# The last 64 keys' values of two head groups in one 64x64 quad, and the first unit's rest rows multiplied in place

## The chip, the cores and the metric

The kernel runs on one core of a Trainium2 chip. Its engines work side by side: TensorE (PE; its weight loads are listed as PEld), VectorE (DVE), ScalarE (ACT) and GpSimd (POOL); SyncE (SP) issues the DMAs. The metric is the time of one execution on the device in microseconds (us), lower is better. Before the change it is 1386.94 us, the median of three runs (1384.19 to 1387.12).

## The reference

Attention with normalised queries and keys, and a feed-forward block with a squared ReLU behind it, all in float32:

```python
q, k, v: (8, 12, 448, 64); g_q, g_k: (64,)
q_n, k_n = rmsnorm(q, g_q), rmsnorm(k, g_k)
attn = softmax(q_n @ k_n^T / sqrt(64))
a = attn @ v                                   # (8, 12, 448, 64)
x = a.transpose(0, 2, 1, 3).reshape(3584, 768)
out = relu(x @ w_in) ** 2 @ w_out              # w_in (768, 2048), w_out (2048, 768)
```

## The kernel before, in words

**Head groups.** A head group `i` is two heads (`e` = 0, 1) of one batch element; there are 8 x 6 = 48. For each group the kernel computes the scores transposed: keys on the 128 partitions, the 448 queries along the row. 448 keys are three chunks of 128 (`m` = 0, 1, 2) and a last one of 64 (`m` = NJ). Since 64 is half a chunk, the last chunks of an even group and of the odd group behind it share one tile: `score` (its matmuls are L444 and L455) writes the even group's to partitions 0 to 63 and the odd group's to 64 to 127, ACT takes the exponential (`weigh`, L463), and both are kept under the even group's key (`key_of`).

**Values.** `attend` (L527) multiplies the exponentials with the values into one PSUM bank, a pair of matmuls per chunk, one for each head (each fills 64 output partitions). For the last chunk the kernel has two ways. In the later units (`joint`, groups from 24 on) `attend_both` (L574) multiplies the shared tile's two halves in four 64x64 quarters of the PE array: the even group's into its own bank, the odd group's into a bank aside, which ACT copies to SBUF (`rests`) and DVE adds later. Before that, each group multiplies the whole shared tile (128 keys) with `lasts[i % 2]`, whose other 64 rows are zero, in a pair of matmuls like the other chunks (L545). `values_of` gives the order of the chunks: an odd group takes the last one first there.

**Stages.** Phase 1 (`visit_alone`) has nothing but attention for the first two batch elements, and weight preparation on DVE, ACT and POOL. A group is visited twice (`n` = 0, 1): scores and exponentials of two chunks, transposes of the next group's q and k (banks 7 and 6), the values of the group before; in the second visit the sums of the exponentials by matmuls with ones (`add_weights`, L594) as well. Then the feed-forward runs in four units (`ffn(u)`), a unit for two batch elements (896 rows), while the attention of the next unit's elements is visited in between (`visit_among` beside the first unit, `visit_whole` beside the later ones). Beside the first unit the sums of the exponentials are added on POOL (`additions`, L482) and their matmul (`denominators`, L611) goes into bank 3, half a visit ahead of the visit. q and k of the next group come in blocks and are transposed on DVE (`turn_blocks`, L367), q is scaled by the gains on ACT (L377).

**Units.** A unit has four blocks of the hidden dimension. The first half of a block is x times w_in (first unit: `first_products`, L1006; later units: `deep_products`, L1062), the second half the hidden rows times w_out (`second_products`, L1260). Both use a scheme of seven products in place of eight on 2x2 blocks (P1 to P7, with forms S1 to S4 of the left and T1 to T4 of the right operand; the S forms are made on POOL, `hidden_sum`, L1171). The second half takes rows in 128s: three tiles (`tt` = 0 to 2) for each of the two batch elements, 2 x 384 of the 2 x 448 rows. The last 64 rows of both elements of a unit are its *rest*, 128 rows that do not fit the 2x2 scheme alone. Before the change, the hidden rests of units 0, 1 and 2 go to DRAM (`keep_rests`, L1179), and the last unit fetches them block by block (`bring_rests`, L1201): rests of units 1 and 2 together make one 2x2 tile more (`tt` = NT), those of units 0 and 3 another (`tt` = NT + 1), seven products each. The last unit's tiles run in the order NT, 0, 1, NT + 1, 2.

**What sets the order.** All instructions are written in order by hand (`manual_schedule`); each engine runs its own in that order. A unit is a generator that yields a cost after each product (18 for a product of the first half of the first unit, 10 for one of the second half). `run(until)` draws products until their cost reaches a mark, and after each one it makes one sum of weight forms (`make_sum`, L1515, DVE and POOL in turn), sends some DMAs, starts a weight conversion if one is due (`late`), and runs a few queued tasks (turns, inverses, additions, normalisations). `place(u, x)` gives the mark of each visit. A conversion (`convert`) is a DMA of words (L1387, L1392), three ACT operations that split them (L1406, L1407, L1409), and on DVE L1420 and L1439 one step later; the conversions of a block end with the second w_out tile, whose T forms are four sums.

In the first unit's cost scale a block is 462 long (252 and 210); visits are marked at thirds of the first and thirds of the second half, and the conversions have eight dates in the second half and eight in the first 160 of the next first half.

## Time and profile before

| | |
|---|---|
| median of three runs | 1386.94 us (1384.19, 1386.94, 1387.12) |
| the profiled execution | 1384.19 us, its span 1382.4 us, granted PE clock 0.999 |
| PE busy | 1358.1 us (98%), 6304 records |
| DVE, ACT, POOL busy | 817.9, 608.7, 804.1 us |
| phase 1 | to about 129.5 us |
| beside the first unit | 129.5 to 480 us, PE busy 343.25 of 350.5 |
| later units with attention | 480 to 1060 us, PE busy 577.52 of 580 |
| the last unit | 1060 to 1382.4 us, PE busy 316.83 of 322.4 |
| values of the last chunk, pairs (L545 on `lasts`) | 96 records, 23.0 us busy |
| values of the last chunk, quads (L580) | 96 records, 14.0 us busy |
| second-half products (L1260) on hid, sums | 800 and 576 records, 285.6 and 205.8 us busy |

A float32 matmul is two records here. Records overlap, so a group's busy time is the union of its records, and the mean of one record is longer than its share of PE's time. In the order of time each line has the start, the length, the engine, the line of the kernel, and what ended the idle time before it in brackets. In a table of stages the columns are the stretch, its length, then busy time and number of instructions of PE, PEld, DVE, ACT and POOL, the granted clock, the DMA share and GB/s.

### The profile page before, as it was taken

How to read it: one execution, taken by the hardware profiler on the slowest of the kernel's cores; microseconds unless marked ns; L12 is line 12 of the kernel's file. 1: busy time of each engine (PE TensorE's matmuls, PEld its weight loads, DVE VectorE, ACT ScalarE, POOL GpSimd, SP SyncE). 2: the span in 40 equal slices, each digit the busy share in tenths (PEclk: the TensorE clock that was granted, in tenths of full speed). 3: DMA queues.
4: the chain of work that ended last, by engine and by line, in shares of the span. 5: the costliest groups of instructions: out<-in, count | busy, mean ns of one | idle time of the engine just before them, and what ended most of it. 6: DMA issues, size and time to landing. Idle time of an engine off the chain costs nothing.

```text
span 1382.4 us, 19667 instructions
## 1 busy us (share of the span) xinstructions
PE 1358.1 (98%) x6304; PEld 844.4 (61%) x6304; DVE 817.9 (59%) x1647; ACT 608.7 (44%) x1122; POOL 804.1 (58%) x810
## 2 busy tenths in 40 slices
PE   7999999999999999999999999999999999999998
PEld 3333444444444585867767675858676968677784
DVE  4786556867767755554557754555547523545454
ACT  6885477767665344333435243433332132202020
POOL 5568764746747886765859875765647440505040
PEclk9999999999999999999999999999999999999999
DMA  5566847869779685756658583847445724334132
GB/s 143 150 158 181 211 124 186 255 185 269 209 188 291 185 237 144 212 141 153 189 154 236 151 241 83 234 113 193 122 140 168 252 65 130 107 104 144 59 122 93
DMA packets 399429, 232.32 MB, mean 168 GB/s; under 512 B 273876, under 2 KB 361044, under 8 KB 398292
## 3 DMA queue, kind: packets, MB, share of 16 engines
q1 hardware_dynamic: 399024, 230.90, 59.4%
q8 instruction: 52, 0.85, 0.3%
q14 instruction: 61, 0.50, 0.1%
q10 hardware_dynamic: 292, 0.07, 0.0%
HBM read 172.49 MB, written 58.39 MB: 167 GB/s over the span
## 4 chain that ended last, share of the span: by engine, by line
PE 82%; DVE 5%; DMA 5%; ACT 3%; SPq 3%; issue 2%; POOL 1%; ACTq 0%; POOLq 0%; DVEq 0%
PE bank L1260 33%; PE bank L1062 25%; PE bank L455 4%; PE bank L559 4%; PE bank L444 4%; PE bank L545 4%; PE bank L1006 3%; DMA words<-in_moe_w_out_dram 2%; DMA qk<-in_k_dram 1%; PE bank L594 1%; DVE more L1475 1%; PE bank L620 1%; SPq L318 1%; DVE acc L1346 1%; PE bank L580 1%
## 5 line engine op out<-in xcount | busy, mean ns | idle before, releaser
L1062 PE MATMUL bank<-xT,in_sb 128*128 128x224 f32 x1344 | 288.2, 353 | 0.0
L1260 PE MATMUL bank<-out_sb,hid 128*128 128x384 f32 x800 | 285.6, 489 | 2.1 <-DVE acc L1346 2.1
L1062 PEld LDWEIGHTS bank<-xT,in_sb 128*128 128x128 f32 x1344 | 252.9, 190 | 10.6 <-ACT wT L463 5.6
L1346 DVE TENSOR_TENSOR acc<-acc,bank 128x384 f32<-128x384 f32 x300 | 160.0, 548 | 146.3 <-PE bank L1260 136.9
L463 ACT ACTIVATE wT<-bank,rr 128x448 f32<-128x448 f32 x288 | 163.9, 631 | 135.1 <-PE bank L444 95.9
L1260 PEld LDWEIGHTS bank<-out_sb,hid 128*128 128x128 f32 x800 | 149.8, 190 | 114.3 <-issue 9.5
L1260 PE MATMUL bank<-out_sb,sums 128*128 128x384 f32 x576 | 205.8, 489 | 1.7 <-DVE acc L1346 1.2
L204 POOL TENSOR_TENSOR rr<-ms,minus_half 128x8 f32<-128x8 f32 (+1 forms) x96 | 147.3, 1535 | 77.9 <-DVE ms L197 69.7
L1047 DVE TENSOR_TENSOR hid<-hid,bank 128x224 f32<-128x224 f32 x312 | 111.3, 384 | 84.9 <-PE bank L1062 79.6
L1260 PEld LDWEIGHTS bank<-out_sb,sums 128*128 128x128 f32 x576 | 108.1, 190 | 83.9 <-DVE acc L1346 4.8
L1006 PE MATMUL bank<-xT,in_sb 128*128 128x448 f32 x336 | 131.9, 546 | 0.3 <-DVE hid L1148 0.3
L1115 POOL TENSOR_TENSOR hid<-hid 128x448 f32<-128x448 f32 x24 | 27.3, 1142 | 176.4 <-DVE hid L1047 172.0
L482 POOL TENSOR_TENSOR sum<-sum,wT 128x448 f32<-128x448 f32 (+1 forms) x96 | 112.4, 1190 | 4.6 <-ACT wT L463 2.9
L455 PE MATMUL bank<-qT,kT 64*128 64x448 f32 (+1 forms) x492 | 104.4, 573 | 3.0 <-ACT qT L377 1.8
L1006 PEld LDWEIGHTS bank<-xT,in_sb 128*128 128x128 f32 x336 | 62.1, 190 | 69.3 <-issue 60.2
L482 POOL TENSOR_TENSOR sum<-wT 128x448 f32<-128x448 f32 x48 | 56.1, 1189 | 66.7 <-ACT wT L463 66.6
L1119 ACT ACTIVATE hid<-hid 128x448 f32<-128x448 f32 x96 | 55.0, 573 | 72.9 <-DVE hid L1047 48.4
L1059 ACT COPY hid<-bank 128x448 f32<-128x448 f32 x24 | 12.8, 533 | 144.6 <-PE bank L1062 144.6
L455 PEld LDWEIGHTS bank<-qT,kT 64*128 64x128 f32 (+1 forms) x492 | 35.6, 167 | 64.7 <-issue 36.2
L444 PE MATMUL bank<-qT,kT 64*64 64x448 f32 x552 | 75.1, 540 | 0.0
L1062 PE MATMUL bank<-more,in_sb 128*128 128x224 f32 x288 | 74.4, 353 | 0.0
L559 PE MATMUL bank<-wT,vt 64*64 64x448 f32 x576 | 73.3, 545 | 0.0
(148 smaller groups left out, 2063.2 us busy)
## 6 DMA issues: line engine op xcount, KB each, us to landing
out_sb<-out_forms SPq DMA_DIRECT2D x80, 384.0 KB, 5.0
in_sb<-in_deep SPq DMA_DIRECT2D x64, 384.0 KB, 4.0
in_sb<-in_deep SPq DMA_DIRECT2D x80, 256.0 KB, 4.0
words<-in_moe_w_in_dram SPq DMA_DIRECT2D x32, 384.0 KB, 4.0
words<-in_moe_w_out_dram SPq DMA_DIRECT2D x32, 384.0 KB, 3.6
out_forms<-out_sb SPq DMA_DIRECT2D x8, 1536.0 KB, 6.0
qk<-in_q_dram SPq DMA_DIRECT2D x96, 96.0 KB, 2.7
qk<-in_k_dram SPq DMA_DIRECT2D x96, 96.0 KB, 2.8
```

The source lines that it names most:

```text
L204: self.nc.gpsimd.tensor_tensor(out=self.rr[i][:, x, 0 : self.count(i)], in0=ms, in1=self.minus_half.to_broadcast(list(ms.shape)), op=ALU.pow,)
L444: nc.tensor.matmul(sc[ds(half * D, D)], lhsT=turned[i, 1][ds(e * D, D), ds(m * P + half * D, D)], rhs=turned[i, 0][ds(e * D, D), :], start ...
L455: nc.tensor.matmul(sc[some], lhsT=turned[p, 1][r, keys], rhs=turned[p, 0][r, :], start=True, stop=True,)
L463: nc.scalar.activation(new_weights((i, m), e), sc, AF.Exp, scale=rows.rr[i][:, 1, 2 * m + e : 2 * m + e + 1],)
L482: nc.gpsimd.tensor_tensor(out=sums[i, e][some], in0=left[some], in1=weights[key_of(i, m), e][some], op=ALU.add)
L545: nc.tensor.matmul(values_bank(i)[ds(e * D, D), :], lhsT=lasts[i % 2][mine, e, :] if m == NJ else values[i][:, m, e, :], rhs=weights[key_o ...
L559: nc.tensor.matmul(bank[ds(e * D, D), :], lhsT=values[i][keys, n, e, :], rhs=weights[(i, n), e][keys], start=n == 0, stop=n == NJ - 1 and ...
L1006: nc.tensor.matmul(ps, lhsT=w_sb[:, IN.index(left), c, :], rhs=forms[u, c][right], start=first and c == 0, stop=c == NK - 1, skip_group_ch ...
L1047: nc.vector.tensor_tensor(out=quarter(name, n), in0=quarter(base, n), in1=ps, op=ALU.add)
L1062: nc.tensor.matmul(ps, lhsT=left, rhs=right, start=start, stop=stop, skip_group_check=True)
L1260: nc.tensor.matmul(ps, lhsT=lefts[left][:, t, ts(tt, P)] if tt < NT else extra[tt - NT][left][:, t], rhs=w_sb[t][:, OUT.index(right), :], ...
L1346: nc.vector.tensor_tensor(out=acc, in0=acc, in1=ps, op=ALU.add)
```

## The change

1. `attend_both` is used for all groups. An even group's last chunk is multiplied together with the odd group's, four matmuls of 64 keys by 64 outputs: the even group's into its values bank, the odd group's into bank 6 in phase 1 and bank 2 beside the first unit. ACT copies that bank to `rests`; when the odd group is finished, DVE adds it to the bank and then multiplies with the inverse. The odd group's own values have three chunks, [0, 1, 2], so its second visit has one pair (beside the first unit) or none (phase 1). The order in which the sums are taken stays (`sums_of`). Both `lasts` tiles are loaded with the even group; their zero halves are no longer written.
2. The rests of the first and of the last unit are multiplied in their own unit by plain products, eight matmuls per block (`multiply_rest`): in the first unit at the head of each second half (three of four parts, then the fourth), in the last unit inside tile 0, whose order is `FIRST_OF_BLOCK`. Units 1 and 2 still keep theirs in DRAM, and the last unit still multiplies them as tile NT; tile NT + 1 is gone. The last unit's tiles run in the order 0, NT, 1, 2. The first and last unit hold one accumulator more.
3. The first unit's block is 502 long (252 and 250) in its cost scale; the visits are marked at equal distances over the whole unit, and the conversions are due every 31.4 without a break.

```diff
     def values_of(i):
         if i % 2:
-            return [0, 1, 2] if joint(i) else [NJ, 0, 1, 2]
+            return [NJ, 0, 1, 2] if shift else [0, 1, 2]
         return [0, 1, 2, NJ]
+
+    def sums_of(i):
+        return [NJ, 0, 1, 2] if i % 2 else [0, 1, 2, NJ]
...
         for n in some:
+            if n >= len(order):
+                continue
             m = order[n]
+            if m == NJ and not shift:
+                attend_both(i)
+                continue
             if joint(i):
-                if m == NJ:
-                    attend_both(i)
-                else:
-                    attend_halves(i, n)
+                attend_halves(i, n)
                 continue
...
     def attend_both(i):
-        other = banks[0][:, 0:S]
+        other = banks[0 if joint(i) else 6 if alone(i) else 2][:, 0:S]
...
         rests[i + 1] = ffn_p.tile([P, S], F32, name="rest", tag="rest", bufs=1)
+        if not joint(i):
+            nc.scalar.copy(rests[i + 1], other)
...
-            nc.vector.tensor_tensor(out=xT, in0=values_bank(i), in1=inverse.pop(i), op=ALU.mult)
+            bank = values_bank(i)
+            if i % 2 and not shift:
+                nc.vector.tensor_tensor(out=xT, in0=bank, in1=rests.pop(i), op=ALU.add)
+                bank = xT
+            nc.vector.tensor_tensor(out=xT, in0=bank, in1=inverse.pop(i), op=ALU.mult)
...
+    FIRST_OF_BLOCK = ["P1", "rest0", "P5", "P4", "P6", "P2", "rest1", "P3", "P7"]
...
-    COST_FIRST, COST_SHORT = 2 * 7 * COST_IN, NT * 7 * COST_OUT
-    COST = NBLK * (COST_FIRST + COST_SHORT)
+    COST_SECOND = (NT * 7 + 4) * COST_OUT
+    COST = NF // 2 * 7 * COST_IN + NBLK * COST_SECOND
+    COST_SHORT = NT * 7 * COST_OUT
     LATER = NBLK * (7 * 11 * COST_DEEP + COST_SHORT)
-    KEPT, REST_PAIRS = range(B // 2 - 1), ((1, 2), (0, 3))
+    KEPT = range(1, B // 2 - 1)
...
+    PARTS = [(0, 0), (1, 0), (0, 1), (1, 1)]
+    PARTS_BY_ROW = [(0, 0), (0, 1), (1, 0), (1, 1)]
+
+    def multiply_rest(u, blk, hid, places, some, acc=None, halves=range(2)):
+        w_sb = [out_sb[n] for n in out_of(u, blk)]
+        for half in halves:
+            ps = places[half][:, 0:HALF]
+            for a, t in some:
+                nc.tensor.matmul(
+                    ps, lhsT=hid[a].rearrange("p t e s -> p t (e s)")[:, t, ds(NT * P, P)],
+                    rhs=w_sb[t][:, 2 * a + half, :],
+                    start=(a, t) == PARTS[0], stop=(a, t) == PARTS[-1],
+                )
+            if acc is not None:
+                add_to(acc[:, ts(half, HALF)], ps, blk == 0)
...
             make_sums(0, 1, 2, 3)
-            later.append([5, lambda: keep_rests(u, blk, hid)])
+            for some in (PARTS[:3], PARTS[3:]):
+                multiply_rest(u, blk, hid, roles, some, accs[-1] if (1, 1) in some else None)
+                yield len(some) * COST_OUT
+            turn_roles(2, 1, 0)
...
-        for tt in () if split else (NT, 0, 1, NT + 1, 2) if final else range(NT):
+        for tt in () if split else (0, NT, 1, 2) if final else range(NT):
             ends = final and blk == NBLK - 1 and tt == NT - 1
-            order = LAST_ORDER if ends else FIRST_ORDER if final and tt == NT else SECOND_ORDER
+            order = LAST_ORDER if ends else SECOND_ORDER if tt or not u else FIRST_OF_BLOCK
             for name in order:
-                product(tt, name, roles[PRODUCTS[name][0]][:, 0:HALF], nc.scalar)
-                if final and (tt, name) == (NT, "P1"):
+                if name.startswith("rest"):
+                    a = int(name[-1])
+                    multiply_rest(
+                        u, blk, hid, banks[2:0:-1], PARTS_BY_ROW[2 * a : 2 * a + 2],
+                        accs[-1] if a else None,
+                    )
...
-    every = ((COST_SHORT - 2 * COST_OUT) / (ahead // 2 - 1), (COST_FIRST - 4 * COST_IN) / (ahead // 2))
+    every = block / ahead
     late = deque(
-        n // ahead * block + (COST_FIRST, block)[m] + 2 + every[m] * (n % (ahead // 2))
-        for n in range(len(all_pieces) - ahead) for m in [n % ahead * 2 // ahead]
+        block + 2 + every * (n - 2 * tile_pieces) for n in range(len(all_pieces) - ahead)
     )
...
     def place(u, x):
         if u == 0:
-            offsets = [COST_FIRST * n // 3 for n in (1, 2, 3)]
-            offsets += [COST_FIRST + COST_SHORT * n // 3 for n in (1, 2, 3)]
-            block = COST // NBLK
+            return COST * x / unit
```

## The prediction

> **What bounds the kernel now.** I read the page's busy times, then the same times by stage, then the order of time of TensorE (PE) in each stage beside the other engines.
>
> ```profile
> PE 1358.1 (98%) x6304; PEld 844.4 (61%) x6304; DVE 817.9 (59%) x1647; ACT 608.7 (44%) x1122; POOL 804.1 (58%) x810
> ```
> ```profile
> 20.00:129.50 109.50, 109.02 (x668) 40.03 (x666) 86.31 (x204) 86.50 (x157) 72.04 (x61) 1.00 0.63 167
> 129.50:480.00 350.50, 343.25 (x1167) 155.63 (x1164) 242.39 (x428) 217.21 (x382) 228.04 (x193) 1.00 0.77 209
> ...
> 1060.00:1382.40 322.40, 316.83 (x1240) 232.78 (x1232) 151.36 (x312) 59.35 (x120) 91.06 (x107) 0.99 0.36 118
> ```
>
> The columns of the stages are length, then busy time of PE, weight loads, DVE, ACT and POOL. PE is full in phase 1 (first row) and in the last unit (third); beside the first unit (second) it is idle for 7 us. So the time is the sum of PE's matmuls plus the few waits, and a matmul taken off PE pays only where nothing else is late at that spot.
>
> The price of a piece of PE work is the distance between the starts of successive pieces in the order of time. Phase 1 first, then one quad as the later units already have it:
>
> ```profile
> 88.69 1.94 PE L455 MATMUL bank<-qT,kT 64*128 64x448 f32 x12
> 90.55 0.97 PE L545 MATMUL bank<-wT,vt 128*64 128x448 f32 x4
> 91.46 0.57 PE L594 MATMUL bank<-wT,ones_of 128*32 128x448 f32 x2
> ...
> 1030.45 1.18 PE L580 MATMUL bank<-wT,lasts 64*64 64x448 f32 x8
> 1031.56 1.02 PE L1062 MATMUL bank<-xT,in_sb 128*128 128x224 f32 x4
> ```
>
> A pair of values matmuls (four records) holds PE for 91.46 - 90.55 = 0.91 us here. Inside a run of pairs it is 0.75 (87.08 to 87.84 in the same order of time), so a pair that stands alone pays some 0.15 for the change of array shape. A quad (eight records) costs 1.11 at the end of a run. Its four matmuls do run side by side, since one after the other would be twice that.
>
> **The change, part by part.**
>
> 1. *Values in phase 1.* Twelve lone or joined pairs of 0.90 go, 10.84 us; six quads come. The nearest row to such a quad is the 64-key score between two other shapes (0.91 from start to start around 89.64); with 0.02 for the shape of the score ahead of it, 0.93. Gain 10.84 - 6 x 0.93 = 5.2 us. The gain falls in the visits of odd groups' values, ahead of the next transposes, which need POOL's scaled q:
>
> ```profile
> 75.53 1.04 POOL L219 TENSOR_TENSOR qk<-qk,rr 128x512 f32<-128x512 f32 x1
> ...
> 76.63 0.55 PE L410 MATMUL bank<-wide,qk 128*128 128x128 f32 x3 [0.15 <-POOL qk L219]
> ```
>
> Scaled q ended at 76.57, PE had to wait. The chain behind it (sums, DVE's inverse, its reduction, POOL's power) starts at the same sums of PE, so moving PE up by 0.9 leaves POOL where it was. At the five transposes that follow a saving, the distance from POOL's end to PE's start (its row and PE's) was 0.9, 1.6, 0.04, 0.45 and 1.4, so about 0.86 + 0.45 = 1.3 us are given back. DVE gets one more add (0.62, by the values row of DVE) per odd group and ACT one copy (0.55). Queued behind the add on DVE are the inverse's users, the next q eviction and the reductions; where the distance was 0.66 and 0.04 (transposes at 103.4 and 121.7) it costs 0.6 more. The copy frees bank 6, which the k transposes need 3 us after the quad, with ACT idle for 2.2 us in one such visit. I give 0.3 for it. Taken: gain 3.0; ends 5.2 and 1.0.
>
> 2. *Values beside the first unit.* Odd groups lose a pair of 0.75 in six visits, right ahead of the 64-key score, and that score waits:
>
> ```profile
> 403.31 0.63 DVE L367 STREAM_TRANSPOSE qT<-qk 128x448 f32<-128x448 f32 x1
> ```
> ```profile
> 402.68 0.59 ACT L1406 ACTIVATE words<-words 128x384 f32<-128x384 f32 x1 [2.56 <-DMA words<-in_moe_w_out_dram]
> ...
> 404.55 0.63 ACT L377 ACTIVATE qT<-qT,g 128x448 f32<-128x448 f32 x1
> ```
> ```profile
> 403.08 1.92 PE L455 MATMUL bank<-qT,kT 64*128 64x448 f32 x8
> 405.24 0.97 PE L455 MATMUL bank<-qT,kT 64*64 64x448 f32 x4 [0.23 <-ACT qT L377]
> ```
>
> The second half of the score starts 0.05 us after ACT has scaled the next group's q, in all six visits (177.39, 232.89, 289.99, 349.52, 405.24, 463.65). That q is set by the last product of the unit, not by the values, so a shorter values step only lengthens the wait. The order of the changed kernel moves the q turn one product (1.29 us) ahead in the two visits that lie in second halves (289.99, 463.65): there the 0.75 is kept and 0.5 of the wait goes, 2.5 together. In two visits (232.89, 405.24) ACT was held by a late weight DMA (2.7 and 2.56 us of idle time); the weight conversions are spread evenly now, and I take back 0.5 each. At 349.52 two DVE operations of a conversion come ahead of the turn: loss 0.5. At 177.39 nothing. Gain 3.0. Even groups: a joined pair (0.75) becomes a quad of 0.91 between two shapes, 6 x 0.16 = 1.0 lost. Net gain 2.0; ends 4.5 and -1.0.
>
> The Trainium skill, TensorEngine Tiling (Array Packing), Key Properties, says that changing the tiling mode drains the array, which speaks against these six quads. The rows (0.91 alone against 0.75 in a run) agree that a change costs, at 0.15 us. If every added change drained a whole matmul of 0.56 us (the mean of one in the values row) the six would lose 3.4 instead of 1.0, and the sum below would end 2.4 us higher.
>
> 3. *The rests.* In the last unit the 56 matmuls of the second rest tile (7 products x 2 x 4 blocks) go and 8 x 4 = 32 plain ones come: 24 fewer. In the first unit 32 more. The chain of waits has this price:
>
> ```profile
> 1184.12 43.86 PE bank L1260 x136
> ```
>
> 43.86 / 136 records = 0.3225, two records to a matmul, 0.645. So +32 x 0.645 = +20.6 and -24 x 0.645 = -15.5, 5.2 us more in all. None of it is hidden: both places are PE's. The copies to DRAM and back that go (8 out, 8 in on SP) cost nothing now and give nothing: SP's wait in the last unit (78.6 us for the rests' tiles) stood behind a finished block, with the weights loaded four pieces ahead.
>
> 4. *Waits in the last unit.* Its blocks used to open with a rest tile whose operands were ready. Now they open with tile 0 in the order that units 1 and 2 already follow: three products before the first sum from POOL. There the 24 records after the opening took 7.83 to 7.96 us, no wait. Ends 0 and 1.1 per block; taken 0.3 in all.
>
> 5. *Waits in the first unit.* (a) The sum of the denominators waited for exponentials that stood behind two weight splits on ACT:
>
> ```profile
> 250.89 1.08 ACT L1409 ACTIVATE words<-words 128x384 f16<-128x384 f32 x1
> 251.71 2.19 ACT L463 ACTIVATE wT<-bank,rr 128x448 f32<-128x448 f32 x4
> ```
> ```profile
> 254.04 0.97 PE L611 MATMUL bank<-sum,ones 128*64 128x448 f32 x4 [0.65 <-ACT wT L463]
> ```
>
> 0.65 here and 1.69 at 339.96. The even spread takes one split of 2.1 us out of the stretch ahead of both: -2.3. (b) Second halves opened with waits for DVE's evictions: 10.69 instead of 9.23 us at 262.26, 0.33 and 0.62 in the next two blocks. Eight rest matmuls (5.36 us) with two adds now stand first: -2.4. At 447.10 four records took 2.93 instead of 1.34, DVE being behind a late DMA; that visit comes 2.6 us later, I take half, -0.8. (c) New: the last weight's T3 and T4 forms of a block are now made on POOL *inside* the second half, behind the four sums and between additions:
>
> ```profile
> 262.97 1.00 POOL L1171 TENSOR_TENSOR sums<-hid 128x384 f32<-128x384 f32 x1 [0.51 <-ACT hid L1155]
> ...
> 266.50 1.12 POOL L1171 TENSOR_TENSOR hid<-hid 128x384 f32<-128x384 f32 x1
> 267.58 2.54 POOL L482 TENSOR_TENSOR sum<-wT 128x448 f32<-128x448 f32 x2
> 270.20 5.05 POOL L482 TENSOR_TENSOR sum<-sum,wT 64x448 f32<-64x448 f32 x4
> ```
>
> From 267.62: two additions 2.54, T3 1.08 (mean of its row), two additions 2.52, T4 1.08 = 274.84, or 12.6 us after the half's start at 262.26. P4, which needs T4, is due after 16 records of rests (5.36) and 16 of P1, P2, P5, P6 (5.16), at 10.5. Wait 2.1. The same sum gives none for the next block (sums end 2.99 after its start) and 1.6 for the last. +3.7; ends 0 (DVE already late there) and +10 (the additions were queued up to 2 us later in each of three blocks, with another wait of the same size behind T3). Net of 5: -1.8.
>
> Sum: -3.0 - 2.0 + 20.6 - 15.5 + 0.3 - 1.8 = -1.4 us against the profiled execution's 1384.19 (span 1382.4 and 1.8 around it), 1382.8. That execution is the fastest of the three; on their median, 1386.94, the same step gives **1385.5**.
>
> **Rivals.**
> *Everything freed is kept.* POOL reaches T4 in time and phase 1's chain moves up with PE: -1.4 - 3.7 - 2.2 = -7.3, 1379.6. For it: POOL has 35% idle time beside the first unit. Against: both chains hang on points that do not move.
> *POOL decides (slower).* One mechanism: T4 behind POOL's additions. Each us that it comes later costs three, one per block after the first. With 2 us more than worked out, +6 - 1.4, 1391.5. It ends slower by 0.2% from 1.4 us more on. For it: POOL's `rr` powers (1.63 each) and scalings lie just ahead of the sums in two of the three blocks. Against: in the trace the sums waited for ACT, not for POOL.
> *The quads do not overlap in their new banks.* Then they save nothing: 12 x 0.75 more, 1394.5. Against: the row at 1030.45.
> *The last unit's blocks wait for the first sums*, 1 us each: 1389.2.
>
> **How the numbers follow.** My case 0.50 (own range 1383 to 1388.5, a third of its spread in parts 1 and 5), all kept 0.18, POOL 0.20, no overlap 0.04, last unit 0.08. About 0.2% (2.8 us) is what a measurement of this kernel tells from no change: below 1384.2 lie nearly all of the first rival and a quarter of my case, 0.30; above 1389.7 three quarters of POOL, the quads, half of the last unit and a little of mine, 0.26; 0.44 between. The range goes from inside the first rival to the POOL case, 1380.5 to 1391.5.
>
> **What would show it.** Right: quads of 0.91 to 1.1 in both stages; the 64-key scores beside the first unit still ended by ACT's scaled q; a wait of 1.5 to 2.5 us ahead of P4 (records on hid after two of sums) in the second and last blocks of the first unit, with POOL's weight form just before; the last unit shorter by 15 us. Wrong: waits at the new rest matmuls, transposes late by more than 1 us in every phase 1 visit, or a first unit more than 22 us longer.

## The result, and the profile after

The changed kernel takes 1378.32 us, the median of nine runs (1377.66 to 1379.21). The kernel before, run as often, takes 1385.1 us. The ratio is 0.9946, with a 95% interval from 0.9934 to 0.9958: the change is a gain of 0.54%, where 1385.5 us, or no difference that can be measured, was forecast. The profiled executions are 1384.19 us before (span 1382.4) and 1377.96 us after (span 1376.2).

The busy times on the page of the changed kernel:

```profile
PE 1351.8 (98%) x6320; PEld 844.0 (61%) x6320; DVE 819.2 (60%) x1647; ACT 614.6 (45%) x1130; POOL 792.1 (58%) x792
```

PE's busy time falls by 6.3 us, as much as the span. There are 16 records (8 matmuls) more than before: the rests add them, and the quads have as many records as the pairs that they replace, but run side by side.

The same stages as before the change, moved to where they now begin and end (phase 1, beside the first unit, the last unit):

```profile
20.00:126.80 106.80, 103.86 (x665) 38.91 (x664) 88.82 (x209) 88.90 (x162) 71.07 (x60) 1.00 0.65 171
126.80:489.00 362.20, 357.79 (x1229) 165.03 (x1225) 250.52 (x444) 222.40 (x389) 229.68 (x194) 1.00 0.74 200
...
1069.60:1376.20 306.60, 300.75 (x1188) 223.75 (x1184) 142.28 (x294) 56.67 (x114) 79.57 (x90) 1.00 0.36 119
```

From border to border in the records of PE, phase 1 is 2.7 us shorter (its end moves from 129.57 to 126.84), the stretch beside the first unit 12.2 us longer (349.91 to 362.15), the later units with attention 0.2 shorter, and the last unit 15.5 shorter (322.02 to 306.55). The forecast had -3.0, +16.8, 0 and -15.2. So it was right in three stages, and the gain came from the fourth: beside the first unit, 4.6 us fewer were added than worked out.

Where? In that stage stand six scores of 64 keys (L455 before, L458 after), each with a step of values right ahead. The second half of such a score uses the next group's q, which DVE turns and ACT scales. From the start of the values to the end of the score, the six took 4.61, 4.82, 4.25, 4.85, 4.71 and 5.31 us before and 4.61, 3.48, 2.77, 5.22, 3.48 and 2.77 after: 6.2 us less, where 3.0 was forecast. The third of them in the order of time of PE, and DVE's turn of q for it, in the kernel before:

```profile
286.64 1.72 PE L545 MATMUL bank<-wT,vt 128*64 128x448 f32 x8
288.29 2.67 PE L455 MATMUL bank<-qT,kT 64*128 64x448 f32 x12
```
```profile
288.61 0.63 DVE L367 STREAM_TRANSPOSE qT<-qk 128x448 f32<-128x448 f32 x1
```

And in the changed kernel:

```profile
291.53 0.97 PE L550 MATMUL bank<-wT,vt 128*64 128x448 f32 x4
292.44 1.94 PE L458 MATMUL bank<-qT,kT 64*128 64x448 f32 x12
294.30 0.91 PE L1286 MATMUL bank<-out_sb,hid 128*128 128x384 f32 x2
```
```profile
291.95 0.63 DVE L370 STREAM_TRANSPOSE qT<-qk 128x448 f32<-128x448 f32 x1
```

In the changed kernel the twelve records of the score run through, 294.30 - 292.44 = 1.86 us, and DVE begins to turn q 0.4 us after the values begin. Before, the score took 2.60 us, DVE began the turn 2.0 us after the values began, and the second half of the score had to wait for the scaled q.

### The profile page after: what moved, and what is told of

Same layout as the page of the kernel before. It is cut to its first block, busy times and chain, and to the rows that moved or that the text cites. A ratio compares the mean times of both kernels' runs of the same rounds, so it can differ in the third digit from the quotient of the medians.

```text
span 1376.2 us, 19610 instructions
## 1 busy us (share of the span) xinstructions
PE 1351.8 (98%) x6320; PEld 844.0 (61%) x6320; DVE 819.2 (60%) x1647; ACT 614.6 (45%) x1130; POOL 792.1 (58%) x792
## 4 chain that ended last, share of the span: by engine, by line
PE 86%; DVE 3%; POOL 3%; issue 2%; ACT 2%; DMA 2%; SPq 1%; POOLq 0%; ACTq 0%; DVEq 0%
PE bank L1286 31%; PE bank L1077 25%; PE bank L1021 8%; PE bank L565 4%; PE bank L447 4%; PE bank L458 4%; PE bank L550 3%; PE bank L1200 2%; PE bank L586 1%; DMA in_sb<-in_deep 1%; PE bank L629 1%; PE bank L602 1%; PE bank L620 1%; DVE acc L1383 1%; SPq L159 1%
## 5 line engine op out<-in xcount | busy, mean ns | idle before, releaser
L1286 PE MATMUL bank<-out_sb,hid 128*128 128x384 f32 x768 | 273.0, 488 | 2.0 <-POOL out_sb L1552 1.4
L1383 DVE TENSOR_TENSOR acc<-acc,bank 128x384 f32<-128x384 f32 x312 | 166.3, 548 | 160.0 <-PE bank L1286 131.4
L1286 PEld LDWEIGHTS bank<-out_sb,hid 128*128 128x128 f32 x768 | 144.6, 190 | 104.4 <-issue 6.3
L458 PE MATMUL bank<-qT,kT 64*128 64x448 f32 (+1 forms) x492 | 102.4, 571 | 3.5 <-ACT qT L380 2.4
L458 PEld LDWEIGHTS bank<-qT,kT 64*128 64x128 f32 (+1 forms) x492 | 35.3, 166 | 63.4 <-issue 37.1
```

What stands on the lines that cost most here:

```text
L458: nc.tensor.matmul(sc[some], lhsT=turned[p, 1][r, keys], rhs=turned[p, 0][r, :], start=True, stop=True,)
L1286: nc.tensor.matmul(ps, lhsT=extra[left][:, t] if tt == NT else lefts[left][:, t, ts(tt, P)], rhs=w_sb[t][:, OUT.index(right), :], start=fi ...
L1383: nc.vector.tensor_tensor(out=acc, in0=acc, in1=ps, op=ALU.add)
```

## The experiments

Two theories at first. **A**: the extra gain beside the first unit comes from when q is ready at those scores, which the new order and the new dates of the conversions changed; a matmul taken off PE there is worth nothing while q is late. **B**: a pair taken off PE is a gain by itself. All times below are medians, each ratio is to the kernel before run on the same chip. This table gives the length of the six scores in the traces that the text uses, in us (1.865 is a score without a wait). A trace is of one execution: "changed, again" is a second trace of the same order of instructions (experiment 3), and it differs from the first by 0.6 us at score 4.

| kernel | 1 | 2 | 3 | 4 | 5 | 6 |
|---|---|---|---|---|---|---|
| before | 2.95 | 3.16 | 2.60 | 3.20 | 3.06 | 3.66 |
| quads only | 3.71 | 4.06 | 3.36 | 4.27 | 3.93 | 4.23 |
| changed, with pairs | 2.96 | 1.865 | 1.865 | 3.57 | 1.865 | 1.865 |
| changed | 3.71 | 2.58 | 1.865 | 4.31 | 2.58 | 1.865 |
| changed, again | 3.71 | 2.58 | 1.865 | 3.71 | 2.58 | 1.865 |
| changed, turn behind a product | 3.71 | 2.58 | 3.07 | 4.10 | 2.58 | 3.51 |
| changed, dates of before | 3.71 | 3.81 | 1.86 | 4.03 | 3.73 | 1.87 |
| changed, early turn | 1.865 | 1.865 | 1.865 | 2.07 | 1.865 | 1.865 |
| before, early turn | 1.865 | 3.18 | 1.865 | 1.865 | 3.44 | 2.75 |
| quads only, early turn | 1.865 | 4.03 | 2.15 | 2.13 | 3.55 | 3.49 |
| changed, dates of before, early turn | 1.865 | 4.02 | 1.865 | 2.14 | 4.04 | 1.865 |
| changed, crowded dates | 3.71 | 2.74 | 2.20 | 3.71 | 2.74 | 1.865 |
| changed, early turn, dates every 26 | 1.865 | 1.865 | 1.865 | 2.38 | 1.865 | 1.865 |

**1. The quads alone.** Part 1 of the change on the kernel before; rests, marks and dates as they were.

```diff
     def values_of(i):
         if i % 2:
-            return [0, 1, 2] if joint(i) else [NJ, 0, 1, 2]
+            return [NJ, 0, 1, 2] if shift else [0, 1, 2]
...
-            nc.vector.tensor_tensor(out=xT, in0=values_bank(i), in1=inverse.pop(i), op=ALU.mult)
+            bank = values_bank(i)
+            if i % 2 and not shift:
+                nc.vector.tensor_tensor(out=xT, in0=bank, in1=rests.pop(i), op=ALU.add)
```

> The kernel before with the quads alone (values, their copy and their add); rests, marks of the visits and dates of the conversions as before. Theory A: what the changed kernel gained beside the first unit at the 64-key scores comes from when the next group's q is turned, not from the quads. So phase 1 is 2.7 us shorter as in the changed kernel, beside the first unit the 64-key scores wait for the scaled q as in the kernel before and take the 0.75 of every pair that is gone, and the six quads cost their 1.0: -1.7 us, ratio 0.9988. Theory B: a pair taken off PE there is a gain by itself, 6.25 us in six visits less 1.0: -8.0 us, ratio 0.9942.

Measured: 1382.93 us, 0.9986 [0.9977, 0.9995]. Phase 1 ends 3.2 us earlier, and beside the first unit nothing is gained (350.43 against 349.91). The values of the odd groups are 0.75 shorter and the scores behind them longer by 0.76, 0.90, 0.76, 1.07, 0.88 and 0.57. The longest row of the waits of PE in that stage, for quads only (what waited, for whom, sum, times, longest):

```profile
PE bank L458 <- ACT qT L380: 6.6, 6, 1.4
```

All six scores wait for ACT's scaled q, as theory A has it.

**2. The changed kernel with pairs.** The same part undone in the changed kernel.

```diff
-            return [NJ, 0, 1, 2] if shift else [0, 1, 2]
+            return [0, 1, 2] if joint(i) else [NJ, 0, 1, 2]
```

> The changed kernel with the pairs and the zero halves of before in place of the quads; rests, marks and dates as changed. Theory A: +2.7 in phase 1, -1.0 for the quads beside the first unit, and a pair more costs 0.75 only in the two visits in second halves whose score no longer waits (+1.5); in the other four the wait for q shrinks by it. +3.3 us against the changed kernel, ratio to the kernel before 0.997. Theory B: +2.7 - 1.0 + 6.25 = +8, ratio 1.0005 to 1.001.

Measured: 1382.07 us, 0.9971 [0.9959, 0.9982]; theory A said 0.997 and B more than 1. Four of the six scores run without a wait; their values step is the long one, as before the change, and in the kernel before they waited. So it is the rest of the change that made q early. Against the changed kernel phase 1 takes 2.3 us more, and the first unit only 0.7.

**3. The turn of q moved.** Two edits of when q may be turned in the changed kernel, one later, one earlier.

```diff
-                run(place(u, x - (1 if whole(i - 1) else 0.5)))
+                run(place(u, x - (1 if whole(i - 1) else 0.5 if not n else 0.44)))
```

> The changed kernel with the point from which the next q may be turned moved from 0.5 to 0.4 of a visit ahead of the visit. In the order of the instructions this takes the turn of q one product later in the two visits that lie in second halves, to where the kernel before has it, and changes nothing at the other four. Theory A: the 64-key scores of these two visits wait again, 1.5 and 2.55 us (the differences between the two traces): +4.0 us against the changed kernel, ratio to the kernel before 0.9975 to 0.998. Theory B: no change, 0.9946.

This run says nothing of the expectation: its edit sets 0.44, as the diff shows, not the 0.4 of the expectation, and with 0.44 every engine has the order of the changed kernel. Its 1378.0 us, 0.9949 [0.9936, 0.9963], is a second measurement of the changed kernel (1378.32). Experiment 7 puts the turn later by another edit.

```diff
-        if in_blocks(i):
+        if in_blocks(i) and first and x == 0:
+            tasks.insert(min(len(tasks), 1), lambda: turn_blocks(i, x))
+        elif in_blocks(i):
             tasks.append(lambda: turn_blocks(i, x))
```

> The changed kernel with the turn of the next q put second in the list of waiting tasks in place of last: q is turned one product earlier in all six visits. Theory A: the waits that are left at the 64-key scores of the changed kernel (2.755, 1.623, 3.361 and 1.624 against 0.912 without a wait, 5.7 us in four visits) go, less what the tasks behind it lose: 3 to 5.7 us faster than the changed kernel, ratio to the kernel before 0.9905 to 0.9925. Theory B: the scores' length there is not set by q; no change, 0.9946.

Measured: 1375.12 us, 0.9929 [0.9916, 0.9943], 3.2 us faster than the changed kernel, at the low end of the 3 to 5.7 expected. Five scores have no wait left and the fourth has 0.2. That gives 5.5 us in the scores; 1.4 of it go to the second halves (their 400 records take 137.1 us, before the edit 135.7), where PE now waits 2.7 us for DVE's evictions, 0.6 before the edit.

**4. The dates of the conversions.** The changed kernel with the dates of the kernel before on the longer block. (The marks at thirds, on halves of 252 and 250, give almost the even marks, so they had nothing to test.)

```diff
-    every = block / ahead
+    half = NF // 2 * 7 * COST_IN // NBLK
+    every = (COST_SECOND - 2 * COST_OUT) / (ahead // 2 - 1), (half - 4 * COST_IN) / (ahead // 2)
     late = deque(
-        block + 2 + every * (n - 2 * tile_pieces) for n in range(len(all_pieces) - ahead)
+        n // ahead * block + (half, block)[m] + 2 + every[m] * (n % (ahead // 2))
+        for n in range(len(all_pieces) - ahead) for m in [n % ahead * 2 // ahead]
     )
```

> The changed kernel (block of 502, quads, rests in place) with the weight conversions dated as the kernel before dates them: eight over the second half, eight over the first 180 of 252 of the next first half. The order of the q turns stays that of the changed kernel. Theory A2: the waits at the 64-key scores depend on how many conversion steps stand on ACT and DVE ahead of the turn of q, so the even dates gave the gain. Then the four scores that the changed kernel has at 2.58, 1.87, 2.58 and 1.87 us go back towards the quads-only kernel's 4.06, 3.36, 3.93 and 4.23 (up to 6.7), the waits of the denominators come back (2.3), and the waits for POOL's T4 form, 3.0, go: up to +6.0 us against the changed kernel, ratio to before 0.997 to 0.999. Theory C: the rest products, which put the visits elsewhere, gave it. Then the scores stay, and it is +2.3 - 3.0, ratio 0.994.

Measured: 1380.47 us, 0.9962 [0.9946, 0.9978], between the two expectations. The waits came back at scores 2 and 5, not at 3 and 6. At score 2, PE and ACT of this kernel, then ACT of the changed kernel in the same place:

```profile
232.74 1.92 PE L458 MATMUL bank<-qT,kT 64*128 64x448 f32 x8
235.65 0.97 PE L458 MATMUL bank<-qT,kT 64*64 64x448 f32 x4 [0.99 <-ACT qT L380]
```
```profile
233.13 0.57 ACT L1443 ACTIVATE words<-words 128x384 f32<-128x384 f32 x1 [2.61 <-DMA words<-in_moe_w_out_dram]
...
234.16 1.07 ACT L1446 ACTIVATE words<-words 128x384 f16<-128x384 f32 x1
234.97 0.63 ACT L380 ACTIVATE qT<-qT,g 128x448 f32<-128x448 f32 x1
```
```profile
231.15 1.07 ACT L1446 ACTIVATE words<-words 128x384 f16<-128x384 f32 x1
233.64 0.67 ACT L380 ACTIVATE qT<-qT,g 128x448 f32<-128x448 f32 x1 [1.42 <-DVE qT L370]
```

With the old dates a conversion (L1443 to L1446) stands just ahead of the scaling (L380): ACT waits 2.61 us for its words, splits them, and gets to q 0.6 us after DVE has turned it. DVE too has a step of a conversion ahead, and turns q 1.87 us after the values begin and not 1.18. With the even dates the split is over by 232.2, and ACT has nothing to do until q is turned. The old dates also brought back a wait of 1.64 us at the denominators (L620), and took the waits at P4 away: the second halves take 133.05 us instead of 135.68.

**5. T4 on DVE.** Those waits at P4 are the one new wait that was forecast. In the changed kernel, second block of the first unit, PE and POOL:

```profile
275.71 0.91 PE L1286 MATMUL bank<-out_sb,hid 128*128 128x384 f32 x2 [0.71 <-POOL out_sb L1552]
```
```profile
271.83 2.75 POOL L485 TENSOR_TENSOR sum<-sum,wT 64x448 f32<-64x448 f32 x2
274.65 1.01 POOL L1552 TENSOR_TENSOR out_sb<-out_sb 128x384 f32<-128x384 f32 x1
```

The form is made behind two additions. This kernel makes it on DVE:

```diff
-            next(sum_engines).tensor_tensor(out=to, in0=left, in1=right, op=op)
+            engine = next(sum_engines)
+            if any(to is some for some in fourths):
+                engine = nc.vector
+            engine.tensor_tensor(out=to, in0=left, in1=right, op=op)
```

> The changed kernel with the T4 form of the last w_out tile of a block made on DVE, not on POOL behind the additions. If the waits at P4 in the first unit (1.57 us in the second block, 1.46 in the last, by the trace) are those for POOL, they go: -3.0 us, ratio to before 0.9924. If DVE's queue, which has the additions into the accumulators there, is as late, or its own readers wait in turn: 0 to -1, ratio 0.994 to 0.9946.

Measured: 1378.38 us, 0.9941 [0.9925, 0.9958], the changed kernel's time. The 36 records that open a second half take 11.81 us in a block without a wait. Over them, the second and the last block lost 0.9 and 0.8 us to waits instead of 1.6 and 1.5, and the third, which had lost none, lost 1.3. DVE and PE in the third:

```profile
362.57 1.48 DVE L1476 CUSTOM_DVE_ANT_0 in_sb<-words,in_sb 128x768 uint16<-128x768 uint16 x1
363.98 0.54 DVE L1383 TENSOR_TENSOR acc<-acc,bank 128x384 f32<-128x384 f32 x1
```
```profile
364.57 1.87 PE L1286 MATMUL bank<-out_sb,hid 128*128 128x384 f32 x4 [0.77 <-DVE acc L1383]
```

A form of 1 us moved from POOL to DVE only moves the wait: evictions take the place of T4.

**6. Both edits, and all rests in DRAM.** The early turn with T4 on DVE; and, on top of both, the rests as before the change (no `multiply_rest`, tile `NT + 1` back) with conversions every 27.1. Of the second, the dates, against the kernel before:

```diff
     late = deque(
-        n // ahead * block + (COST_FIRST, block)[m] + 2 + every[m] * (n % (ahead // 2))
-        for n in range(len(all_pieces) - ahead) for m in [n % ahead * 2 // ahead]
+        n // ahead * block + COST_FIRST + 2 + (COST_SHORT - 2 * COST_OUT) / 7 * (n % ahead)
+        for n in range(len(all_pieces) - ahead)
     )
```

> The changed kernel with both: q turned one product earlier (measured alone: -2.9 us) and T4 on DVE. If the two waits are independent, the gains add: -5.9 us against the changed kernel, ratio to before 0.9905. If DVE, which gets both, decides: no better than the early q alone, 0.993.

> The quads, even marks, early q and T4 on DVE, but all rests kept in DRAM and multiplied by the seven-product scheme in the last unit, as in the kernel before; conversions every 27.1 of a block of 462. It has 8 plain matmuls fewer (32 + 32 plain less 56), 8 x 0.645 = 5.2 us. If the openings of the second halves and the last unit lose nothing by it, 5.2 us faster than the changed kernel with early q and T4 on DVE, ratio to before 0.987. If the second halves wait again for DVE's evictions (2.4 us in the kernel before) and the denominators for the exponentials (2.3), only 0.5 better, ratio 0.990.

The first: 1374.58 us, 0.9911 [0.9895, 0.9928], 0.5 us below the early turn alone. Whether the two add stays open: the ratio is near the 0.9905 of a full sum, but the intervals of this kernel and of the early turn alone (0.9929) overlap, and the traces speak against it. There the first unit is 359.47 us, with the early turn alone 358.10: the wait for T4 (0.6) is gone, and PE's waits for DVE's evictions are 3.7 us instead of 2.7. The second: 1392.86 us, 1.0043 [1.0029, 1.0058], slower than the kernel before, where both expectations had it fastest. The last forms of a block's weights are now made inside the second half, with no rest products ahead of the tiles, and PE waits there for weight forms on DVE (4.0 us in all), for evictions on DVE (3.8) and for S forms on POOL (2.6): 336 records took 130.35 us, against 114.45 with the quads alone and the early turn (experiment 8). That kernel has other marks, other dates and T4 on POOL, and which of the three makes the difference was not separated.

**7. The turn behind one more product.** An empty task ahead of the turn: on DVE, q is turned behind the eviction of one more product, as in the order of before; on PE, ACT and POOL nothing moves, and on SP some loads change places.

```diff
         if in_blocks(i):
+            if first and x == 0:
+                tasks.append(lambda: None)
             tasks.append(lambda: turn_blocks(i, x))
```

> The changed kernel with an empty task ahead of the turn of q. In the order of DVE this puts the turn behind the eviction of one more product of a second half (in four visits; with a conversion step in three of them) and changes the order of no other engine but SP. Theory A2: the 64-key scores wait for what stands on DVE and ACT ahead of the turn. Then the two scores that have no wait now (1.865 us) and the two at 2.58 take 3 to 4 us, +4 to +6.7 us against the changed kernel, ratio to before 0.9975 to 0.9995. If another thing (the load of q's blocks, the place of the rest products) sets the turn, the scores stay: 0.9946.

Measured: 1380.66 us, 0.9961 [0.9948, 0.9975], 2.3 us slower than the changed kernel, less than the 4 to 6.7 that the theory had. Scores 3 and 6 got their waits back, 1.21 and 1.65 us. The other two turns that moved are of q that no score is waiting for, so two scores moved and not four. At score 3 the turn begins 1.7 us after the values and not 0.4. At the sixth, DVE and PE:

```profile
470.46 0.55 DVE L1307 TENSOR_TENSOR acc<-acc,bank 128x384 f32<-128x384 f32 x1
471.01 0.55 DVE L1383 TENSOR_TENSOR acc<-acc,bank 128x384 f32<-128x384 f32 x1
...
473.02 0.65 DVE L370 STREAM_TRANSPOSE qT<-qk 128x448 f32<-128x448 f32 x1 [0.18 <-DMA qk<-in_q_dram]
```
```profile
474.42 0.97 PE L458 MATMUL bank<-qT,kT 64*64 64x448 f32 x4 [0.69 <-ACT qT L380]
```

In the changed kernel the turn followed the L1307 row and began within 0.03 us of the values. Here one more eviction and two operations of a deep form (left out) stand between, and the turn begins 2.1 us after the values; 0.18 of that is a wait for the load of q. That is the step of the forecast, shown by undoing it.

**8. What a pair is worth when q is early.** The early turn on the kernel before, and on the quads alone; and on the kernel of experiment 4.

> The kernel before with the early turn of q and nothing else. Its six scores take 2.953, 3.164, 2.600, 3.197, 3.056 and 3.660 us, 18.6, so 7.4 us of waits can go: ratio 0.9947, with a third given back 0.9964. Against the run of the quads with the early turn it prices the quads where q is not late: by theory A2 a pair taken off PE is then kept, 3.2 in phase 1 and 6 x 0.75 - 1.0 = 3.5 beside the first unit, a difference of 6.7 us; if the pairs there are eaten by something else, a difference of 2.7 us as without the early turn.

> The quads alone (rests, marks and dates as before) with the turn of q put second in the list of tasks. In the quads-only kernel the six scores took 3.711, 4.062, 3.355, 4.269, 3.934 and 4.234 us, 23.6, against 6 x 1.865 = 11.2 without a wait. If the early turn ends all six waits and delays nothing else: -12.4 us against quads only, ratio to before 0.9897; with a third given back to the tasks that now come later, as in the changed kernel with the early turn, -8, 0.993. If the next limit is near (DVE's evictions), -4, 0.996.

> The changed kernel with the conversion dates of before and the early turn of q. With the dates of before the trace had no wait at P4 (-3.1 us against the changed kernel), but waits at the scores (+2.4) and ahead of the denominators (+1.7). The early turn takes the waits at the scores away: against the changed kernel with the early turn -3.1 + 1.7 = -1.4 us, ratio to before 0.992. If the conversions hold the early turn back as they held the late one: 0.994 or more.

Measured: 1382.08 us, 0.9967 [0.9956, 0.9978]; 1376.32 us, 0.9931 [0.9918, 0.9945]; 1377.08 us, 0.9933 [0.992, 0.9947]. With the early turn the quads are worth 1382.08 - 1376.32 = 5.8 us; without it, by the medians of experiment 1, 1385.23 - 1382.93 = 2.3. The traces show where. Values and score together are 0.75, 0.46 and 0.49 us shorter with the quads at scores 1, 3 and 4, which have no wait with the pairs; at 2 and 6, where q is late in both, they gain nothing (+0.10 and -0.01). At 5 they gain 0.64 although q is late in both. So in five of six places a pair beside the first unit is gained where q is not late and lost where it is, as theory A says. With the dates of before, scores 2 and 5 stay at 4.0 us even with the early turn: there DVE has turned q by 1.1 us after the values begin, and ACT begins to scale it 2.3 us later, behind a conversion. The quads with all rests kept are as fast as the changed kernel with the early turn (0.9931 and 0.9929), though PE has 8 matmuls fewer: in the first unit the rests cost 358.10 - 343.83 = 14.3 us and not the 21.1 of their own records. The comparison changes the dates and marks too, so what part of the 6.8 is cover by the rests stays open.

**9. Place or density of the conversions.** Dates that leave the stretch ahead of scores 2 and 5 free and end early, but stand densely; without and with the early turn.

```diff
+    dates = [2 + every * n for n in range(-2 * tile_pieces, 0)]
+    dates += [2, 17, 32, 90, 105, 120, 135, 150]
     late = deque(
-        block + 2 + every * (n - 2 * tile_pieces) for n in range(len(all_pieces) - ahead)
+        (1 + n // ahead) * block + dates[n % ahead] for n in range(len(all_pieces) - ahead)
     )
```

> The changed kernel with other dates for the eight w_out conversions of a block (2, 17, 32, 90, 105, 120, 135, 150 after the block's start, in place of every 31.4 from 2 to 222): none lies in the stretch from half a visit ahead of the second visit of a block (42) to that visit (84), and the last ends well before the second half. Theory A2 (a conversion between the turn's mark and the visit holds the scaled q, and a late last conversion holds P4): the scores that are at 2.575 us in the changed kernel stay at 2.6 or less, where the dates of the kernel before gave 3.81 and 3.73, and the waits at P4 (3.0 us) are gone; the rest as in the changed kernel, less what five conversions in a row delay ahead of the denominators (0 to 1.7): -1.3 to -3.0 us against the changed kernel, ratio to before 0.9925 to 0.9935. If it is the density of the conversions and not their place, the two scores go to 3.7 and more and it is 0 to +1: 0.9946 to 0.9955.

> The same dates and the early turn of q. The two gains lie at different places (P4 in the second halves; the 64-key scores): if they add, -3 us against the changed kernel with the early turn (0.9929), ratio to before 0.9905 to 0.992. If the conversions that now crowd behind the second visit take it back, 0.993.

Measured: 1386.11 us, 1.0005 [0.9996, 1.0014]; 1381.42 us, 0.9973 [0.9964, 0.9982]. What the first expectation said of its places held nearly: scores 2 and 5 are at 2.74, and the second halves have no waits at P4 (132.45 us). The sums did not, in either kernel: the first has 6.5 us more beside the first unit than the changed kernel. There PE waits for other things on ACT. Ahead of the first of these rows ACT has split two weights (the last step, L1446, begins at 254.50 and takes 1.07), and the exponentials that PE needs come behind, from 255.32 to 257.49:

```profile
257.64 0.97 PE L620 MATMUL bank<-sum,ones 128*64 128x448 f32 x4 [1.92 <-ACT wT L466]
258.54 6.47 PE L1021 MATMUL bank<-xT,in_sb 128*128 128x448 f32 x12
```
```profile
345.00 2.61 PE L1021 MATMUL bank<-xT,in_sb 128*128 128x448 f32 x3 [3.28 <-ACT part L1030]
```

And a wait here costs more than its length: see the last section. PE's waits beside the first unit add up to 7.9 us instead of 4.4, and the lower clock behind these two costs 3.1 more, which is about the 6.5. So place decides at those scores, and density, by these rows, elsewhere; of the dates run, the even spread serves both.

**10. Nearly even dates.** Every 26 in place of 31.4 for the eight w_out conversions, with the early turn.

```diff
+    dates = [2 + (every if n < 0 else 26) * n for n in range(-2 * tile_pieces, 2 * tile_pieces)]
```

> The changed kernel with the early turn of q, and the eight w_out conversions of a block every 26 in place of every 31.4 (the last at 184 in place of 222): the spread of the dates stays nearly even, and the last weight is ready some 38 of cost, about two products of a first half, earlier. If the waits at P4 hang on the last conversion alone, they go (1.6, 2.3 and 1.3 us over the time of 36 records in the second halves of the kernel with the early turn, 5 in all, of which 3.0 as in the changed kernel are P4's): -3 us against the early turn alone (0.9929), ratio to before 0.9905. If each step nearer to the dates of before brings back the waits of the denominators (1.7 at one or two places) it is -1.5 to 0, 0.992 to 0.993.

Measured: 1372.75 us, 0.9909 [0.9893, 0.9926], 2.4 us below the early turn alone by the medians (0.9929), near the first expectation; the intervals overlap, and the profiled executions differ by 1.4. The waits of PE beside the first unit in this kernel:

```profile
PE bank L1286 <- DVE acc L1383: 2.3, 2, 1.5
PE bank L620 <- ACT wT L466: 0.9, 1, 0.9
```

Nothing waits for T4 (POOL out_sb) any more: the 36 records that open a second half take 11.81 us in all four blocks. Of the scores only the fourth is late, by 0.5 us. Its median is the lowest of all kernels run, 12.4 us below that of the kernel before; by the ratio it is not told from the early turn with T4 on DVE (0.9911).

## Why the prediction was wrong

Its sum was -1.4 us; the profiled executions differ by -6.2. A further 1.8 us of the distance between 1385.5 and 1378.32 is the base: the sum was put on the median of three runs, 1386.94, and nine runs have 1385.1.

| step | predicted | measured |
|---|---|---|
| 1. values in phase 1 | -3.0 | -2.7 |
| 2. values beside the first unit, odd groups | -3.0 | -6.2 |
| 2. the six quads there | +1.0 | +0.96 |
| 3. rests, first unit | +20.6 | +21.1 |
| 3. and 4. last unit | -15.2 | -15.5 |
| 5a. denominators | -2.3 | -2.5 |
| 5b. openings; 447.10 | -2.4; -0.8 | -2.3; -1.6 |
| 5c. T4 | +3.7 | +3.0 |

- *Step 1 held in its sum, by luck in part.* A quad takes 0.91 from start to start, and the transposes wait for POOL's scaled q as was said, 1.05 us at 74.72. But PE's waits for POOL there grew from 0.4 to 2.9 us, 2.5 where 1.3 was worked out; in return no wait of PE for DVE's add or ACT's copy shows, for which 0.9 had been taken.
- *Step 2 failed, in size.* It was given 3.0 us and measured 6.2; the 3.2 us between are two thirds of the difference between the two sums. The mechanism was the right one: the scores wait for ACT's scaled q, and a saved pair only lengthens the wait (experiment 1). The visits were named rightly too: nothing at the first, and gains at the second, third, fifth and sixth. The loss forecast for the fourth (0.5) is not shown: it is 0.37 in one trace of the changed kernel, and the second trace has a gain of 0.24 there. For the third and sixth "the 0.75 is kept and 0.5 of the wait goes, 2.5 together"; they gave 1.49 and 2.55, 4.0. The working let q come one product earlier but kept part of the wait. In fact q came 1.6 and 3.0 us earlier against the start of the values, and all of the wait went; undoing only the place of the turn takes 2.9 of the 4.0 back (experiment 7). For the second and fifth "I take back 0.5 each" from the even conversions; they gave 1.34 and 1.23, since the 1.2 us for which the conversion had held the score went whole (experiment 4).
- *The quads.* They were worth what the rows said: +0.96 for six. The price by which each would drain the array for a whole matmul, 3.4, is refuted here.
- *Steps 3 and 4 held.* The 32 rest matmuls take 0.658 each (5.265 for 16 records), and the openings of the last unit's blocks have no wait.
- *Step 5.* (a) held. In (b) the opening at 447.10 lost all of its 1.6 us of waiting (2.93 instead of 1.34), not half. (c) held: 1.57, 0 and 1.46 us are lost at P4, where 2.1, 0 and 1.6 were worked out. A first part of each ends with an eviction on DVE (0.33 and 0.23 in brackets), the last with POOL's form (0.71 and 0.69).
- *The rivals.* "Everything freed is kept", at 1379.6, came nearest, but for other reasons than its own: POOL did not reach T4 in time, and phase 1's chain did not move up. "POOL decides" would have needed T4 1.4 us later; the waits for it were 0.1 to 0.5 shorter than worked out. So the nearness of the first rival is luck. That the result lay so far from the main case came most of all from taking a part of a wait at four scores, where the trace gave the distance of q from the score.

## What to carry to other kernels

Where PE stands in front of an operand that another engine makes late, work taken off PE is worth nothing, and moving the operand is worth all: here nothing for the six pairs of experiment 1, and 3 us for one task put earlier in a list. So measure, for each such place, the distance from the operand's end to the moment when PE could use it, and ask of a change first what it does to that distance; a wait that is shorter than the shift goes whole, not by half. Background work with due times (here conversions) did best in these runs when it was spread evenly, with the last one early enough: crowded dates removed the waits that they were chosen for and made longer ones.

## What was not expected of the hardware

A wait of PE can cost nearly twice its length. In the first kernel of experiment 9, by windows (length, then busy time and records of PE, weight loads, DVE, ACT and POOL; the granted clock is third from the end):

```profile
258.50:260.00 1.50, 1.50 (x5) 0.83 (x4) 0.98 (x3) 1.32 (x3) 1.50 (x3) 0.72 1.11 308
260.00:262.00 2.00, 2.00 (x4) 0.81 (x3) 1.97 (x5) 1.16 (x2) 2.00 (x2) 0.50 1.06 258
```

After the wait of 1.92 us at 257.64 the granted clock falls to 0.50 for some 3.4 us, and the twelve records of the product behind it take 6.40 us instead of 4.71: 1.7 us more. After the wait of 3.28 us at 345.00 it falls too, and four records take 3.03 us instead of 1.61. In the kernel with all rests in DRAM it came after two waits close together, 0.61 and 1.24 us (ending at 262.66 and 264.82), and in waits of 2.59 and 1.06 us (355.46 and 357.43). The waits of up to 1.72 us that stood alone (in the second kernel of experiment 9 at 254.89, in the kernel before 1.69 at 339.96) left the clock at 1.00. So did two of 1.06 and 1.07 us close together in the kernel with all rests in DRAM (445.33 and 447.93). What decides between these cases is not shown. The Trainium skill, TensorE: Matmul & The Clock Gate (Why this matters for your kernels), asks for no idle gaps over about 3 us between bursts of matmuls. Here one of 1.92 was enough.
